# Gate splits on VectorE, down projections a step sooner, and next-layer inputs at the head of a step

## The chip, the cores and the metric

The kernel runs on one NeuronCore of a Trainium2 chip. The metric is the device time of one execution in microseconds. Three runs of the kernel before gave 650.26, 651.15 and 651.91 us, so the median is 651.15 us.

## What is computed

Local attention over blocks is followed by two feed-forward layers without a residual path. The first layer gates with a cosine, the second with Mish:

```python
def _moe_ref(x, w_in, w_out):          # layer 1 of the kernel's l = 0
    h = x @ w_in                        # 1536 x 512 @ 512 x 2048
    g = h * np.cos(h)
    return g @ w_out                    # 2048 x 512

def _moe2_ref(x, w_in, w_out):          # l = 1
    h = x @ w_in
    sp = np.where(h > 20.0, h, np.log1p(np.exp(np.minimum(h, 20.0))))
    return (h * np.tanh(sp)) @ w_out

x = attention(q, k, v)                  # 2 batches, 8 heads, 768 tokens, 64 wide
out = _moe2_ref(_moe_ref(x, ...), ...)
```

The attention part ends some 120 us after the start and is the same in both kernels.

## The kernel before

**Numbers in two halves.** TensorE multiplies in a rounded 32-bit format, so every operand is kept as a rounded upper half and a lower half, which is the value minus the upper half. Each product is made of three matmuls: upper by upper, lower by upper, upper by lower. The layer input X has the halves `xh` and `xl`, the weights `wih`, `wil`, `woh`, `wol`, and the gated activations `gh` and `gl`.

**Stages and steps.** A layer's 2048 hidden columns are cut into 4 groups `g` of 512, and the 1536 tokens into 3 blocks `j` of 512. A stage is one layer, group and block, so there are 24 stages: 0 to 11 for layer 0, 12 to 23 for layer 1. A stage has 4 tiles `f` of 128 hidden columns, so there are 96 tiles, and the loop over `k` in `layers()` makes one step per tile. In step k TensorE runs `up(k)`, 12 matmuls (L139) that make h of the tile in one of four banks, and then one `down(s, u)`, 12 matmuls (L555) that multiply the four gated tiles of a finished stage s with a quarter u of the output weights. A down needs all four `gh` and `gl` of its stage; the eleventh of its matmuls is the one that reads the last tile's `gl`.

**The gate of layer 0** spreads over two steps. In step k, `turns` makes n on ScalarE (L521) and r on VectorE in two instructions (L522, L523). In step k + 1, `cos_gate` takes the sine on ScalarE (L527) and multiplies on VectorE (`gg`, L529), and `split` makes `gh` on ScalarE (L514) and `gl` (L515). In layer 0 `gl` is made on GpSimd, in layer 1 on VectorE.

**Downs and what follows them.** When the last tile of a stage is split in step k, its four downs go into the list `downs` with a due step, k + 2 in layer 0 and k + 1 in layer 1 (`LAG`), and `do_down` takes one per step. In the step after a down, `do_after` adds its bank into `acc`, on ScalarE for g = 0 (L562) and on VectorE otherwise (L564). For the last group (g = 3), an `end` runs one step later still: in layer 0 it makes `xh` (L569, ScalarE) and `xl` (L570, GpSimd), which are the input of layer 1, and in layer 1 it stores the result.

**Weights for the next group** arrive meanwhile, eight chunks per group of 12 steps. The weights are 64-bit numbers, and each chunk is narrowed by one ScalarE instruction (L101) and three VectorE instructions (L105, L108, L111) in one step, and split in the next step by ScalarE (L121) and GpSimd (L122, `wil` or `wol`). Eight steps in twelve carry this load on VectorE; they are called heavy below, the others plain.

**The order** on each engine is the order of the program, written out by hand; nothing reorders it. One step issues on VectorE: `gg` of the tile before, the add, the two r of this tile, then the three narrowing instructions. Tile 43, for instance, is the last of stage 10; its `gg` is made in step 44 and written gg(43) below.

Of the kernel before, what the change touches and what calls it, by code (L numbers as in the profile page):

```python
# [9 lines left out]
F32 = mybir.dt.float32  # L10
# [4 lines left out]
ALU = mybir.AluOpType  # L15
# [5 lines left out]
def kernel(  # L21
# [11 lines left out]
    nc = tc.nc  # L33
# [8 lines left out]
    KD = DM // 128  # L42
# [5 lines left out]
    TPB = TB // 128  # L48
# [78 lines left out]
    stages = [(l, g, j) for l in range(2) for g in range(NG) for j in range(NBLK)]  # L127
    tiles = [(s, f) for s in range(len(stages)) for f in range(GF)]
    HP = {}

    def up(k, half=None):
        s, f = tiles[k]
        l, g, j = stages[s]
        w = W[l, g][0]
        ps = HP[k] = BANK[k % 4][:, 0:TB]
        n = 6 if half == 1 else 0
        for c in range(KD) if half is None else range(2 * half, 2 * half + 2):
            for a, e in PASS:
                nc.tensor.matmul(ps, lhsT=w[a][:, c, 128 * f:128 * f + 128],  # L139
                                 rhs=X[e][:, c, TB * j:TB * j + TB], start=(n == 0), stop=(n == 3 * KD - 1))  # L140
                n += 1
# [359 lines left out]
    def layers():  # L501
        with ExitStack() as es:
            gp = es.enter_context(tc.tile_pool(name="g", bufs=10))
            tp = es.enter_context(tc.tile_pool(name="tmp", bufs=3))
            ap = es.enter_context(tc.tile_pool(name="acc", bufs=NBLK))
            G, ACC = {}, {}

            def tmp(nm, bufs=3, dt=F32):
                return tp.tile([128, TB], dt, tag=nm, name=nm, bufs=bufs)

            def split(g, eng):

                hi, lo = [gp.tile([128, TB], F32R, tag="g" + a, name="g" + a) for a in "hl"]
                nc.scalar.copy(hi, g)  # L514
                eng.tensor_tensor(out=lo, in0=g, in1=hi.bitcast(F32), op=ALU.subtract)  # L515
                return hi, lo

            def turns(h):

                n, r = tmp("n", 2, I32), tmp("r")  # L520
                nc.scalar.activation(out=n, in_=h, func=AF.Identity, scale=1.0 / TWO_PI, bias=b_quarter)  # L521
                nc.vector.scalar_tensor_tensor(out=r, in0=n, scalar=-C1, in1=h, op0=ALU.mult, op1=ALU.add)  # L522
                nc.vector.scalar_tensor_tensor(out=r, in0=n, scalar=-C2, in1=r, op0=ALU.mult, op1=ALU.add)  # L523
                return h, r

            def cos_gate(h, r):
                nc.scalar.activation(out=r, in_=r, func=AF.Sin, bias=b_hpi)  # L527
                g = tmp("gg")
                nc.vector.tensor_tensor(out=g, in0=r, in1=h, op=ALU.mult)  # L529
                return g  # L530

            def mish(h):
                g = tmp("gg")
                nc.scalar.activation(out=g, in_=h, func=AF.Mish)  # L534
                return split(g, nc.vector)

            turn = [0]

            def dbank():
                turn[0] += 1  # L540
                return BANK[4 + turn[0] % 4]

            def down(s, u, d0=0, d1=DM):
                l, g, j = stages[s]
                w = W[l, g][1]
                if l == 0:
                    ps = dbank()[:, 0:TB]
                    mm = [(w[a][:, f, 128 * u:128 * u + 128], G[s, f][e]) for f in range(GF) for a, e in PASS]
                    col = slice(TB * u, TB * u + TB)
                else:  # L550
                    ps = dbank()[:, 0:d1 - d0]
                    mm = [(G[s, f][a][:, 128 * u:128 * u + 128], w[e][:, f, d0:d1]) for f in range(GF) for a, e in PASS]
                    col = slice(DM * u + d0, DM * u + d1)
                for n, (x, y) in enumerate(mm):
                    nc.tensor.matmul(ps, lhsT=x, rhs=y, start=(n == 0), stop=(n == len(mm) - 1))  # L555
                if u == 0 and g == 0:
                    ACC[l, j] = ap.tile([128, KD * TB], F32, tag="acc", name="acc")
                acc = ACC[l, j][:, col]

                def add():  # L560
                    if g == 0:
                        nc.scalar.copy(acc, ps)  # L562
                    else:
                        nc.vector.tensor_tensor(out=acc, in0=acc, in1=ps, op=ALU.add)  # L564

                def end():
                    if l == 0:
                        hi, lo = (y[:, u, TB * j:TB * j + TB] for y in X)
                        nc.scalar.copy(hi, acc)  # L569
                        nc.gpsimd.tensor_tensor(out=lo, in0=acc, in1=hi.bitcast(F32), op=ALU.subtract)  # L570
                    else:
                        r0 = TB * j + 128 * u
                        nc.sync.dma_start(out=out[r0:r0 + 128, d0:d1], in_=acc)

                return [add, end] if g == NG - 1 else [add]

            downs, after = [], [[], []]
            LAG = (2, 1)

            def do_after():  # L580
                now = after.pop(0)
                after.append([])
                for op in now:
                    op()

            def do_down(k):
                if downs and downs[0][0] <= k:
                    for x, op in zip(after, down(*downs.pop(0)[1:])):
                        x.append(op)

            def made(k, i, g):

                s, f = G_OF = tiles[i]
                G[G_OF] = g
                if f == GF - 1:
                    downs.extend((k + LAG[stages[s][0]], s, u) for u in range(KD if stages[s][0] == 0 else TPB))
                    if s == len(stages) - 1:
                        downs[-1:] = [(k, s, TPB - 1, 256 * h, 256 * h + 256) for h in range(2)]

            st = {}  # L600
            for k in range(len(tiles) + 12):
                if k < len(tiles):
                    if k not in HP:
                        up(k)
                    h = HP.pop(k)
                g = cos_gate(*st.pop(k - 1)) if k - 1 in st else None
                do_after()
                first = k < len(tiles) and stages[tiles[k][0]][0] == 0
                if first:
                    st[k] = turns(h)  # L610
                if g is not None:
                    made(k, k - 1, split(g, nc.gpsimd if first else nc.vector))
                if k < len(tiles) and not first:
                    made(k, k, mish(h))
                for op in WSEQ.get(tiles[k] if k < len(tiles) else None, ()):
                    op()
                do_down(k)
                if k >= len(tiles):
                    do_down(k + 99)
            do_after()  # L620
            do_after()

    groups = [(l, g) for l in range(2) for g in range(NG)]
    WSEQ = {}
# [26 lines left out]
    with tc.manual_schedule():  # L651
        def filler(i):
            for op in AT.get(i, ()):
                op()
            if NS <= i < NS + 6:
                up((i - NS) // 2, (i - NS) % 2)
        attention(filler)
        layers()
# [30 lines left out]
```

## Time and profile before

| | us |
|---|---|
| median of 3 runs | 651.15 |
| the profiled execution | 650.98 |
| its span, first to last instruction | 649.2 |
| outside the span | 1.8 |
| TensorE busy | 632.3 (97%) |
| VectorE busy | 440.9 (68%) |
| ScalarE busy | 320.2 (49%) |
| GpSimd busy | 236.8 (36%) |

The busy time of TensorE counts overlapping matmuls as they are pipelined, so 97% says only that there is nearly always a matmul in flight. What TensorE loses shows in two ways: as idle time ahead of a matmul, with the engine that ended it, and as fewer matmuls in a stretch of equal length. VectorE's 68% is a mean over layer 0, where it is busy nearly all the time, and layer 1, where it is not. Rows of the trace name an engine, a line of the kernel, the operation, what it writes and reads, and after a bracket how long the engine was idle and who ended that.

### The profile page before, as it was taken

The page shows a single profiled execution, that of the slowest core. Times are in us where ns is not written, and L with a number is a line of the kernel's source. Part 1 is how long each engine was busy: PE and PEld are TensorE (multiplying, and loading weights), DVE is VectorE, ACT ScalarE, POOL GpSimd, SP SyncE. Part 2 cuts the span into 40 slices and gives each one's busy share as a digit, 9 for nine tenths or more (in the row PEclk, how much of TensorE's full clock was granted, in tenths as well). Part 3 has the DMA queues.
Part 4 walks back from the last instruction along what each step waited for, and adds up shares of the span by engine and source line. Part 5 has one row for each costly group of instructions (what it writes and reads, how often), then busy time and mean ns, then how long its engine had stood idle before and what let it go on. Part 6 is the DMA issues. An engine that isn't in the chain of part 4 may idle for free.

```text
span 649.2 us, 8827 instructions
## 1 busy us (share of the span) xinstructions
PE 632.3 (97%) x3096; PEld 515.1 (79%) x3097; DVE 440.9 (68%) x813; ACT 320.2 (49%) x701; POOL 236.8 (36%) x279
## 2 busy tenths in 40 slices
PE   9998999999999999999999699999999999999998
PEld 4766778888878888888888588888888888888886
DVE  5698986488988989998999848622563366322222
ACT  5787897565565445544545545543543244322210
POOL 5466568255555443544355624310221022100000
PEclk9999999999999999999999799999999999999999
DMA  9969652022213211221122102311221122000112
GB/s 184 205 158 212 146 140 67 2 65 91 76 61 98 89 41 34 96 97 34 46 86 78 53 28 74 116 43 34 80 101 47 32 72 92 1 0 1 48 50 97
DMA packets 54410, 49.88 MB, mean 77 GB/s; under 512 B 44270, under 2 KB 44526, under 8 KB 54126
## 3 DMA queue, kind: packets, MB, share of 16 engines
q1 hardware_dynamic: 54366, 49.32, 27.2%
q8 instruction: 24, 0.39, 0.3%
q14 instruction: 20, 0.16, 0.1%
HBM read 45.57 MB, written 3.15 MB: 75 GB/s over the span
## 4 chain that ended last, share of the span: by engine, by line
PE 55%; DVE 32%; issue 6%; ACT 5%; POOL 1%; DMA 1%; DVEq 0%; ACTq 0%; POOLq 0%
PE bank L555 23%; PE bank L139 21%; PE bank L210 11%; DVE wx L105 6%; DVE wx L108 6%; DVE gg L529 4%; DVE r L523 4%; DVE r L522 3%; DVE acc L564 3%; DVE wx L111 2%; ACT r L527 1%; ACT wx L101 1%; DMA wst<-in_moe_w_in_dram 1%; ACT wih L121 1%; DVE vb L210 1%
## 5 line engine op out<-in xcount | busy, mean ns | idle before, releaser
L139 PE MATMUL bank<-xh,wih 128*128 128x512 f32 x384 | 150.6, 392 | 4.4 <-ACT xh L569 4.4
L139 PE MATMUL bank<-xl,wih 128*128 128x512 f32 x384 | 149.8, 390 | 0.6 <-POOL xl L570 0.6
L139 PE MATMUL bank<-xh,wil 128*128 128x512 f32 x384 | 149.7, 390 | 0.0
L515 POOL TENSOR_TENSOR gl<-gg,gh 128x512 fp32r<-128x512 f32 x47 | 67.8, 1442 | 132.6 <-ACT gh L514 106.6
L515 DVE TENSOR_TENSOR gl<-gg,gh 128x512 fp32r<-128x512 f32 x49 | 34.2, 697 | 115.2 <-ACT gh L514 115.1
L534 ACT ACTIVATE gg<-bank 128x512 f32<-128x512 f32 x48 | 28.7, 598 | 149.3 <-PE bank L139 147.9
L514 ACT CAST gh<-gg 128x512 fp32r<-128x512 f32 x96 | 59.6, 621 | 75.7 <-DVE gg L529 74.2
L139 PEld LDWEIGHTS bank<-xh,wih 128*128 128x128 f32 x384 | 72.2, 188 | 20.1 <-ACT xh L569 4.8
L139 PEld LDWEIGHTS bank<-xl,wih 128*128 128x128 f32 x384 | 72.2, 188 | 15.8 <-POOL xl L570 1.1
L139 PEld LDWEIGHTS bank<-xh,wil 128*128 128x128 f32 x384 | 72.2, 188 | 15.0
L122 POOL TENSOR_TENSOR wil<-wx,wih 128x512 fp32r<-128x512 f32 x32 | 46.4, 1450 | 88.8 <-ACT wih L121 84.6
L555 PE MATMUL bank<-gl,woh 128*128 128x512 f32 x192 | 75.7, 394 | 1.3 <-POOL gl L515 1.1
L105 DVE TENSOR_SCALAR wx<-wx 128x512 int32<-128x512 int32 x64 | 66.8, 1043 | 13.5 <-ACT wx L101 13.5
L555 PE MATMUL bank<-gh,woh 128*128 128x512 f32 x192 | 75.4, 393 | 0.0
L555 PE MATMUL bank<-wol,gh 128*128 128x512 f32 (+1 forms) x196 | 75.4, 385 | 0.0
L555 PE MATMUL bank<-woh,gl 128*128 128x512 f32 (+1 forms) x196 | 75.4, 385 | 0.0
L555 PE MATMUL bank<-woh,gh 128*128 128x512 f32 (+1 forms) x196 | 75.4, 385 | 0.0
L555 PE MATMUL bank<-gh,wol 128*128 128x512 f32 x192 | 75.3, 392 | 0.0
L210 POOL TENSOR_TENSOR pn<-pb,rs 128x256 f32<-128x256 f32 (+3 forms) x120 | 53.7, 472 | 38.2 <-PE bank L210 14.1
L564 DVE TENSOR_TENSOR acc<-acc,bank 128x512 f32<-128x512 f32 (+1 forms) x73 | 49.3, 675 | 26.0 <-PE bank L555 26.0
L122 POOL TENSOR_TENSOR wol<-wx,woh 128x512 fp32r<-128x512 f32 x32 | 47.3, 1477 | 49.4 <-ACT woh L121 40.8
L108 DVE SCALAR_TENSOR_TENSOR wx<-wst,wx 128x512 int32<-128x512 int32 x64 | 62.3, 973 | 1.9
(78 smaller groups left out, 1004.2 us busy)
## 6 DMA issues: line engine op xcount, KB each, us to landing
wst<-in_moe_w_in_dram SPq DMA_DIRECT2D x32, 512.0 KB, 3.5
wst<-in_moe_w_out_dram SPq DMA_DIRECT2D x32, 512.0 KB
kn<-in_k_dram SPq DMA_DIRECT2D x16, 192.0 KB, 4.0
qn<-in_q_dram SPq DMA_DIRECT2D x16, 192.0 KB, 3.8
vn<-in_v_dram SPq DMA_DIRECT2D x16, 192.0 KB, 3.1
out_dram<-acc SPq DMA_DIRECT2D x11, 256.0 KB, 2.0
vb<-in_v_dram SPq DMA_DIRECT2D x2, 960.0 KB, 7.4
vt<-in_v_dram SPq DMA_DIRECT2D x32, 18.8 KB, 3.0
```

What stands on the lines that cost most here:

```text
L105: nc.vector.tensor_scalar(out=xi, in0=xi, scalar1=3, scalar2=0x7FFFFFF8, op0=ALU.logical_shift_left, op1=ALU.bitwise_and)
L108: nc.vector.scalar_tensor_tensor(out=xi, in0=word[:, :, 0], scalar=29, in1=xi, op0=ALU.logical_shift_right, op1=ALU.bitwise_or)
L122: nc.gpsimd.tensor_tensor(out=lo, in0=x, in1=hi.bitcast(F32), op=ALU.subtract)
L139: nc.tensor.matmul(ps, lhsT=w[a][:, c, 128 * f:128 * f + 128], rhs=X[e][:, c, TB * j:TB * j + TB], start=(n == 0), stop=(n == 3 * KD - 1))
L210: todo[phase].append(lambda: fn(*a, **kw))
L514: nc.scalar.copy(hi, g)
L515: eng.tensor_tensor(out=lo, in0=g, in1=hi.bitcast(F32), op=ALU.subtract)
L523: nc.vector.scalar_tensor_tensor(out=r, in0=n, scalar=-C2, in1=r, op0=ALU.mult, op1=ALU.add)
L529: nc.vector.tensor_tensor(out=g, in0=r, in1=h, op=ALU.mult)
L534: nc.scalar.activation(out=g, in_=h, func=AF.Mish)
L555: nc.tensor.matmul(ps, lhsT=x, rhs=y, start=(n == 0), stop=(n == len(mm) - 1))
L564: nc.vector.tensor_tensor(out=acc, in0=acc, in1=ps, op=ALU.add)
```

## The change

Three things change in `layers()`.

- `split` makes `gl` on VectorE always, so in layer 0 it leaves GpSimd and stands on VectorE behind the two r of the step.
- The downs of stage 0 keep their two steps' distance; those of all other stages are due from one step behind the last split (`late`), each with its own due step, and up to two that are due run in a step. Stage 1 becomes due while the last down of stage 0 does, so step 9 has two downs, and from there on layer 0 is one down ahead of before. Step 52, at the border of the layers, has two as well, and layer 1 is then two downs ahead of before until its end.
- `do_after` is parted: the adds stay behind `gg`, and the ends go to the head of the step, ahead of the sine.

```diff
-            def split(g, eng):
+            def split(g):
                 hi, lo = [gp.tile([128, TB], F32R, tag="g" + a, name="g" + a) for a in "hl"]
                 nc.scalar.copy(hi, g)
-                eng.tensor_tensor(out=lo, in0=g, in1=hi.bitcast(F32), op=ALU.subtract)
+                nc.vector.tensor_tensor(out=lo, in0=g, in1=hi.bitcast(F32), op=ALU.subtract)
                 return hi, lo
...
-            downs, after = [], [[], []]
-            LAG = (2, 1)
-            def do_after():
-                now = after.pop(0)
-                after.append([])
-                for op in now:
+            downs, adds, ends = [], [], [[], []]
+            def do_adds():
+                while adds:
+                    adds.pop(0)()
+            def do_ends():
+                for op in ends.pop(0):
                     op()
-            def do_down(k):
-                if downs and downs[0][0] <= k:
-                    for x, op in zip(after, down(*downs.pop(0)[1:])):
-                        x.append(op)
+                ends.append([])
+            def do_downs(k):
+                for _ in range(2):
+                    if downs and downs[0][0] <= k:
+                        add, *end = down(*downs.pop(0)[1:])
+                        adds.append(add)
+                        ends[1].extend(end)
...
-                    downs.extend((k + LAG[stages[s][0]], s, u) for u in range(KD if stages[s][0] == 0 else TPB))
+                    late = 2 if s == 0 else 1
+                    downs.extend((k + late + u, s, u) for u in range(KD if stages[s][0] == 0 else TPB))
                     if s == len(stages) - 1:
-                        downs[-1:] = [(k, s, TPB - 1, 256 * h, 256 * h + 256) for h in range(2)]
+                        downs[-1:] = [(k + TPB, s, TPB - 1, 256 * h, 256 * h + 256) for h in range(2)]
...
                     h = HP.pop(k)
+                do_ends()
                 g = cos_gate(*st.pop(k - 1)) if k - 1 in st else None
-                do_after()
+                do_adds()
...
-                    made(k, k - 1, split(g, nc.gpsimd if first else nc.vector))
+                    made(k, k - 1, split(g))
...
-                do_down(k)
-                if k >= len(tiles):
-                    do_down(k + 99)
+                do_downs(k if k < len(tiles) else k + 99)
```

On VectorE, step 6, a heavy one of stage 1, before:

```order
L529 TENSOR_TENSOR gg<-r,bank_59 128x512
L522 SCALAR_TENSOR_TENSOR r<-n,bank_60 128x512
L523 SCALAR_TENSOR_TENSOR r<-n,r 128x512
L105 TENSOR_SCALAR wx<-wx 128x512
L108 SCALAR_TENSOR_TENSOR wx<-wst,wx 128x512
L111 SCALAR_TENSOR_TENSOR wx<-wst,wx 128x512
L529 TENSOR_TENSOR gg<-r,bank_60 128x512
```

and step 6 after the change:

```order
L529 TENSOR_TENSOR gg<-r,bank_59 128x512
L522 SCALAR_TENSOR_TENSOR r<-n,bank_60 128x512
L523 SCALAR_TENSOR_TENSOR r<-n,r 128x512
L515 TENSOR_TENSOR gl<-gg,gh 128x512
L105 TENSOR_SCALAR wx<-wx 128x512
L108 SCALAR_TENSOR_TENSOR wx<-wst,wx 128x512
L111 SCALAR_TENSOR_TENSOR wx<-wst,wx 128x512
L529 TENSOR_TENSOR gg<-r,bank_60 128x512
```

`gl` now stands between the second r and the narrowing, where VectorE had nothing of it before.

On TensorE at the end of step 9, where the last down of stage 0 (bank_62) ends, before:

```order
L555 MATMUL bank_62<-gh,woh 128x512
L555 MATMUL bank_62<-gl,woh 128x512
L555 MATMUL bank_62<-gh,wol 128x512
L139 MATMUL bank_60<-xh,wih 128x512
L139 MATMUL bank_60<-xl,wih 128x512
L139 MATMUL bank_60<-xh,wil 128x512
```

and after, where the first down of stage 1 (bank_63) follows at once and `up(10)` (bank_60) comes 12 matmuls later:

```order
L555 MATMUL bank_62<-gh,woh 128x512
L555 MATMUL bank_62<-gl,woh 128x512
L555 MATMUL bank_62<-gh,wol 128x512
L555 MATMUL bank_63<-gh,woh 128x512
L555 MATMUL bank_63<-gl,woh 128x512
L555 MATMUL bank_63<-gh,wol 128x512
```

From here on every down of layer 0 stands one place sooner among the ups than before.

On ScalarE, steps 46 and 47 before (n of step 46 reads bank_60, n of step 47 bank_61); the second `xh` is the last of token block 0 (stage 9, u = 3), which `up(48)`, the first of layer 1, reads:

```order
L101 ACTIVATE wx<-wst 128x512
L527 ACTIVATE r<-r,b_hpi 128x512
L569 CAST xh<-acc 128x512
L521 ACTIVATE n<-bank_60,b_quarter 128x512
L514 CAST gh<-gg 128x512
L121 CAST woh<-wx 128x512
L527 ACTIVATE r<-r,b_hpi 128x512
L569 CAST xh<-acc 128x512
L521 ACTIVATE n<-bank_61,b_quarter 128x512
```

and after, step 45 and the head of step 46, where the second `xh` is that same last one:

```order
L569 CAST xh<-acc 128x512
L527 ACTIVATE r<-r,b_hpi 128x512
L521 ACTIVATE n<-bank_59,b_quarter 128x512
L514 CAST gh<-gg 128x512
L121 CAST woh<-wx 128x512
L101 ACTIVATE wx<-wst 128x512
L569 CAST xh<-acc 128x512
L527 ACTIVATE r<-r,b_hpi 128x512
L521 ACTIVATE n<-bank_60,b_quarter 128x512
```

The last `xh` of the block moved from step 47, behind the sine, to step 46, ahead of it.

## Rows read from the trace of the kernel before

**Rows 1.** Groups by line: matmuls with xh and with gl; idle before, and releaser.

```profile
L139 PE MATMUL bank<-xh,wih 128*128 128x512 f32 x384 | 150.6, 392 | 4.4 <-ACT xh L569 4.4
...
L555 PE MATMUL bank<-gl,woh 128*128 128x512 f32 x192 | 75.7, 394 | 1.3 <-POOL gl L515 1.1
```

**Rows 2.** Busy time by stretch (PE, PEld, DVE, ACT, POOL), PEclk, DMA: attention, layers' border.

```profile
60.00:80.00 20.00, 17.11 (x124) 13.54 (x120) 17.49 (x69) 16.71 (x59) 10.38 (x21) 0.91 0.62 141
...
360.00:380.00 20.00, 15.07 (x55) 11.58 (x54) 13.85 (x18) 10.51 (x17) 10.54 (x8) 0.83 0.09 26
380.00:400.00 20.00, 20.00 (x90) 16.57 (x89) 13.60 (x17) 9.42 (x17) 7.22 (x5) 1.00 0.19 55
...
366.10:373.00 6.90, 5.42 (x12) 3.94 (x13) 5.46 (x7) 4.48 (x8) 4.52 (x4) 0.51 0.00 0
```

**Rows 3.** Timeline at the border: start, length, engine, line, out<-in, idle before.

```profile
363.01 0.68 DVE L564 TENSOR_TENSOR acc<-acc,bank 128x512 f32<-128x512 f32 x1
...
366.36 0.60 ACT L569 CAST xh<-acc 128x512 fp32r<-128x512 f32 x1
...
367.02 0.79 PE L139 MATMUL bank<-xh,wih 128*128 128x512 f32 x1 [4.36 <-ACT xh L569]
...
368.38 0.79 PE L139 MATMUL bank<-xl,wih 128*128 128x512 f32 x1 [0.57 <-POOL xl L570]
```

**Rows 4.** Timeline, VectorE in a plain step of layer 0.

```profile
239.20 0.69 DVE L529 TENSOR_TENSOR gg<-r,bank 128x512 f32<-128x512 f32 x1 [0.86 <-ACT r L527]
...
241.12 1.34 DVE L523 SCALAR_TENSOR_TENSOR r<-n,r 128x512 f32<-128x512 int32 x1
...
243.32 0.69 DVE L529 TENSOR_TENSOR gg<-r,bank 128x512 f32<-128x512 f32 x1 [0.86 <-ACT r L527]
```

**Rows 5.** Timeline, VectorE and GpSimd in a heavy step of layer 0.

```profile
270.62 0.68 DVE L529 TENSOR_TENSOR gg<-r,bank 128x512 f32<-128x512 f32 x1
...
272.53 1.40 DVE L523 SCALAR_TENSOR_TENSOR r<-n,r 128x512 f32<-128x512 int32 x1
273.86 1.52 DVE L105 TENSOR_SCALAR wx<-wx 128x512 int32<-128x512 int32 x1
...
276.75 0.68 DVE L529 TENSOR_TENSOR gg<-r,bank 128x512 f32<-128x512 f32 x1
...
272.09 1.30 POOL L515 TENSOR_TENSOR gl<-gg,gh 128x512 fp32r<-128x512 f32 x1 [3.12 <-issue]
273.35 1.74 POOL L122 TENSOR_TENSOR wil<-wx,wih 128x512 fp32r<-128x512 f32 x1
```

**Rows 6.** Timeline, the same VectorE operations where no GpSimd operation was running ahead.

```profile
178.48 0.69 DVE L523 SCALAR_TENSOR_TENSOR r<-n,r 128x512 f32<-128x512 int32 x1
...
250.62 0.41 DVE L105 TENSOR_SCALAR wx<-wx 128x512 int32<-128x512 int32 x1
...
378.08 0.69 DVE L515 TENSOR_TENSOR gl<-gg,gh 128x512 fp32r<-128x512 f32 x1 [1.90 <-ACT gh L514]
```

**Rows 7.** Timeline, gg of tile 7 and the first matmul of down(1, 0).

```profile
154.01 0.68 DVE L529 TENSOR_TENSOR gg<-r,bank 128x512 f32<-128x512 f32 x1
...
154.68 0.39 PE L555 MATMUL bank<-gh,woh 128*128 128x512 f32 x1
```

**Rows 8.** Timeline, steps 44 to 46: matmuls behind up(44) and up(46), VectorE before gg(43).

```profile
341.41 0.39 PE L555 MATMUL bank<-gh,woh 128*128 128x512 f32 x1
...
345.75 1.72 DVE L108 SCALAR_TENSOR_TENSOR wx<-wst,wx 128x512 int32<-128x512 int32 x1
...
348.11 0.68 DVE L529 TENSOR_TENSOR gg<-r,bank 128x512 f32<-128x512 f32 x1
...
352.29 0.39 PE L555 MATMUL bank<-gh,woh 128*128 128x512 f32 x1
```

**Rows 9.** Timeline, TensorE behind two other idle times.

```profile
62.31 0.85 PE L210 MATMUL bank<-ident,pn 128*128 128x128 f32 x3 [2.06 <-ACT pt L210]
...
180.35 0.50 PE L555 MATMUL bank<-gl,woh 128*128 128x512 f32 x1 [1.07 <-POOL gl L515]
```

More of the change, by code (lines that the diff above doesn't have):

```diff
@@ L534, in mish @@
                 nc.scalar.activation(out=g, in_=h, func=AF.Mish)
-                return split(g, nc.vector)
+                return split(g)
             turn = [0]
@@ L616, in layers @@
                     op()
-                do_down(k)
-                if k >= len(tiles):
-                    do_down(k + 99)
-            do_after()
-            do_after()
+                do_downs(k if k < len(tiles) else k + 99)
+            do_adds()
+            do_ends()
+            do_ends()
     groups = [(l, g) for l in range(2) for g in range(NG)]
```

## Prediction

> **What bounds the kernel now.** I read the groups by line first, for TensorE's idle time in the layers and who ends it. There are only two places [rows 1]: 4.4 us ahead of a matmul with xh, and 1.3 us in all ahead of matmuls with gl. Then the busy time by stretch, for what the first place costs: from 360 to 380 us TensorE ran 55 matmuls, from 380 to 400 us 90 [rows 2]. The 35 missing ones, at 20 / 90 = 0.222 us, are 7.8 us. That is more than the idle time, because from 366.1 to 373 us the granted clock is 0.51, the level of 1.2 GHz, after it had been at 2.4 GHz until TensorE stood idle [rows 2]. Everywhere else in the layers TensorE runs at its pace: a step is 24 matmuls, and (352.29 - 341.41) / 2 = 5.44 us [rows 8], so half a step, an up or a down, is 2.72 us.
>
> The timeline then shows why TensorE stood idle [rows 3]. up(48) needs the last xh and xl of token block 0. VectorE's add of that part is at 363.01, the end with xh on ScalarE at 366.36, one step later and behind a sine, and TensorE goes on at 367.02 and, with xl, at 368.38. So VectorE is late, not TensorE. Its own pace shows in two kinds of step. From gg to gg a heavy step takes 276.75 - 270.62 = 6.13 us [rows 5], over TensorE's 5.44; a plain one takes 243.32 - 239.20 = 4.12 us, 0.86 of it waiting for the sine [rows 4]. Eight heavy and four plain steps are 65.5 us against 12 x 5.44 = 65.3 us. VectorE is level with TensorE over a group and runs behind it by a few us, until the extra GpSimd work of the ends makes heavy steps longer and the border comes.
>
> **What gl on VectorE costs.** It adds 0.69 us to each of 47 steps [rows 6]. What it takes away is in the lengths of other VectorE instructions. The second r takes 0.69 us alone [rows 6], but 1.34 to 1.40 where GpSimd's gl started just before it [rows 4, 5]; L105 takes 0.41 alone [rows 6] and 1.52 under GpSimd's wil [rows 5]. In both cases the VectorE instruction ends some 0.3 to 0.55 us behind GpSimd's: it waits until GpSimd is done. So two GpSimd operations in a heavy step hold VectorE up by 0.71 + 1.11 = 1.8 us. With gl gone from GpSimd one operation of about 1.3 us is left to hold up one VectorE instruction, about 1.1 us, and gl adds 0.7: 1.8 us again. A heavy step stays near 6.1 us. In a plain step no GpSimd operation is left, so the second r is 0.65 us shorter, and gl fits into the 0.86 us in which VectorE waits for the sine. That makes 4.12 - 0.65 = 3.45 us. Four plain steps win 2.6 us per group, so VectorE catches up with TensorE in each group and starts the heavy steps without delay.
>
> The Trainium skill (GPSIMD Engine Reference, section 1) says that GpSimd shares its memory interfaces with VectorE and contends with VectorE instructions that have two inputs in SBUF. The new gl is such an instruction. By that rule it can itself be held up by the weights' split; the trace agrees as far as the second r goes.
>
> **The downs a step sooner.** The count of matmuls is the same, so this costs only where a down now comes before its gl. The eleventh matmul of a down reads the last gl, 2.27 us after the first.
>
> Stage 1: down(1, 0) began at 154.68 [rows 7]; now up(10) is behind it, so it begins at 151.96 and wants gl at 154.2. gg(7) was at 154.01 [rows 7]. Steps 4 to 7 each save up to about 0.4 us (L105 1.1 shorter, gl 0.7 longer), so gg(7) lies between 152.4 and 154.0. gl follows behind two r: gg, r, r and gl without hindrance end 2.6 us after gg begins, and 3.7 us after if wil comes first. gl is then ready between 155.0 and 157.7, and TensorE waits 0.8 to 3.5 us; I take 1.8, nearer the low end because L105's saving is measured. Once TensorE is that much later, stage 2 fits almost: 0.1.
>
> Stages 3 to 9: VectorE starts each group level. Stage 7 is the tightest. From step 27, where VectorE is level, five heavy steps are 5.8 + 4 x 6.1 = 30.2 us against 5 x 5.44 = 27.2, so gg(31) begins 3.0 us behind the end of up(32). gl comes 4.4 us later (one add more than above, wil first), at 7.4; down(7, 0) follows up(33), so it is wanted at 5.44 + 2.27 = 7.7. That is about even; I take 0.1, bounds 0 and 0.5.
>
> Stage 10: the ends of stage 9 add xl to GpSimd, and L108 is 1.72 us there [rows 8], about 1.1 more per step. Before, gg(43) began 348.11 - 341.41 = 6.7 us behind up(44). Now, level at step 39, five heavy steps, two of them longer, are 3 x 6.0 + 2 x 7.2 = 32.4 us against 27.2, so gg(43) begins 5.2 us behind up(44), and gl is there 3.3 to 4.4 us later, at 8.5 to 9.6. down(10, 0) follows up(45), so its gl is wanted at 5.44 + 2.27 = 7.7. TensorE waits 0.8 to 1.9 us; if VectorE is not level at step 39, up to 3; I take 1.4. Behind that stall stage 11 has its gl in time.
>
> **The border of the layers.** The last down of stage 9 is in step 44, its add in step 45, its end at the head of step 46. With gg(44) 7.2 us behind gg(43), the end's xh is made some 2.4 us after gg(44), ahead of the sine, and xl behind one wol, about 5.7 us after gg(44): 5.2 + 7.2 + 5.7 = 18.1 us behind up(44). up(48) wants it at 3 x 5.44 + 2.72 + 2.27 + 1.4 = 22.7. A margin of over 4 us: the wait goes, and with it the slow clock behind it. What is late next is gl for the downs, as above. In layer 1 a down comes two places sooner. There gh and gl follow the up within three instructions, and the down has another half step and an up before it; no cost. GpSimd's 47 operations of gl were beside other work but for the holding up already counted. The last matmuls and stores keep their order.
>
> **Sum.** Gone: 7.8 + 1.3 = 9.1 us. New: 1.8 + 0.1 + 0.1 + 1.4 = 3.4 us. 650.98 - 9.1 + 3.4 = 645.3 for the profiled execution, which holds the 649.2 us span and 1.8 us around it, neither of them touched outside the layers; it lies 0.17 under the median of 651.15, so 645.5 us.
>
> **Rivals.** (1) The clock falls in the new waits. Behind 4.36 us idle it was at 1.2 GHz for 6.9 us [rows 2, 3]. Behind 1.07 us the next matmul took 0.50 us against 0.79 at the border, so it held; behind 2.06 us in the attention [rows 9] it fell, since that stretch has 0.91 [rows 2]. Mine are 1.8 and 1.4. A fall like the border's costs 6.9 us x (1 - 0.51) = 3.3 us: 648.8 for one, 652 for two. The Trainium skill (TensorE: Matmul & The Clock Gate, What's actually happening) says that the slow clock is the default and that activity lifts it; the border's rows agree, and by that rule alone any new wait is suspect.
> (2) Slower: the second r and gl are both held up, or wil falls between them, so that gl costs its 0.7 us in heavy steps and nothing comes back. A heavy step is then 6.8 us, a group 8 x 6.8 + 4 x 3.45 = 68.2 us against 65.3, and VectorE sets layer 0: 4 x 2.9 = 11.6 us, with 1.8 at stage 1, less the 9.1: about 655.5. It decides from a heavy step of some 6.7 us. For it speaks that gl on VectorE never ran beside a weights' split in the trace; against it that two hold-ups become one.
> (3) No wait to speak of is left, gl coming first every time: 642 to 643.
> (4) The border's wait stays in part, because block 0's xl still queues on GpSimd behind the splits, or the edits cancel: about 650. The order speaks against it, since xh stands a whole step sooner.
>
> **How the numbers follow.** A measurement can tell about 0.3%, 2 us, from no change: faster is below 649.2, slower above 653.1. The forecast, 643.3 to 647.8, has 0.58; rival 3 0.10; rival 1 0.17, of which 0.12 below 649.2; rival 4 0.07; rival 2 0.08. So faster is 0.80, same 0.12, slower 0.08. The range runs from 642.3, into rival 3, to 649.5, over most of rival 1.
>
> **What would show it.** After: no idle ahead of matmuls with xh, 90 matmuls in each 20 us across the border, PEclk 1.00 there. TensorE's idle time ahead of matmuls with gl grows from 1.3 to about 3.4 us, now released by VectorE, at stages 1 and 10. Second r in plain steps 0.69 us, plain steps 3.5 us, heavy ones 6.1. I am wrong if heavy steps exceed 6.5 us, or if PEclk is under 1 near stages 1 or 10.

## The result and the profile after

The changed kernel takes 644.47 us (median of 4 runs, 644.08 to 645.08) against 651.53 us for the kernel before (4 runs, 650.26 to 652.07). The ratio is 0.9895, with a 95% interval of 0.9878 to 0.9912: 1.05% faster, about 7 us. The profiled execution took 644.43 us, with a span of 642.7 us. The 651.15 us given for the kernel before is the median of three of its four runs.

TensorE's groups by line in the changed kernel (busy, mean ns, then the idle time before them and who ended it), against [rows 1]:

```profile
L139 PE MATMUL bank<-xh,wih 128*128 128x512 f32 x384 | 150.2, 391 | 0.0
...
L555 PE MATMUL bank<-gl,woh 128*128 128x512 f32 x192 | 74.9, 390 | 2.1 <-DVE gl L515 2.1
```

The 4.4 us ahead of a matmul with xh are gone. The idle time ahead of matmuls with gl grew from 1.3 to 2.1 us and is now ended by VectorE. Busy time by stretch of the changed kernel (PE, PEld, DVE, ACT, POOL, PEclk, DMA), against [rows 2]:

```profile
140.00:160.00 20.00, 19.22 (x84) 15.45 (x83) 19.59 (x27) 11.41 (x21) 5.94 (x4) 1.00 0.28 87
...
340.00:360.00 20.00, 18.67 (x82) 15.14 (x82) 19.69 (x24) 10.26 (x18) 9.19 (x6) 1.00 0.24 80
360.00:380.00 20.00, 20.00 (x90) 16.54 (x89) 16.21 (x22) 11.80 (x19) 9.20 (x6) 1.00 0.08 26
```

Across the border, from 360 to 380 us, TensorE runs 90 matmuls instead of 55, at a granted clock of 1.00 instead of 0.83. What is left lies in the two other stretches. The timeline of TensorE in the changed kernel shows both places, with the first matmul of the waiting down and the first of the up that follows it, for the second place:

```profile
155.62 0.50 PE L555 MATMUL bank<-gl,woh 128*128 128x512 f32 x1 [0.78 <-DVE gl L515]
...
349.34 0.39 PE L555 MATMUL bank<-gh,woh 128*128 128x512 f32 x1
...
353.09 0.50 PE L555 MATMUL bank<-gl,woh 128*128 128x512 f32 x1 [1.33 <-DVE gl L515]
...
353.67 0.39 PE L139 MATMUL bank<-xh,wih 128*128 128x512 f32 x1
```

These are down(1, 0) and down(10, 0), the two that the prediction named. The second takes 353.67 - 349.34 = 4.33 us instead of 2.72, so an idle time of 1.33 us loses 1.6.

VectorE in a plain step of the changed kernel, against [rows 4], and in step 44 with the GpSimd work beside it, against [rows 5, 8]:

```profile
231.10 0.68 DVE L529 TENSOR_TENSOR gg<-r,bank 128x512 f32<-128x512 f32 x1
231.69 0.68 DVE L564 TENSOR_TENSOR acc<-acc,bank 128x512 f32<-128x512 f32 x1
232.29 0.68 DVE L522 SCALAR_TENSOR_TENSOR r<-n,bank 128x512 f32<-128x512 int32 x1
233.00 0.69 DVE L523 SCALAR_TENSOR_TENSOR r<-n,r 128x512 f32<-128x512 int32 x1
233.61 0.69 DVE L515 TENSOR_TENSOR gl<-gg,gh 128x512 fp32r<-128x512 f32 x1
234.49 0.69 DVE L529 TENSOR_TENSOR gg<-r,bank 128x512 f32<-128x512 f32 x1 [0.19 <-ACT r L527]
...
348.75 0.68 DVE L529 TENSOR_TENSOR gg<-r,bank 128x512 f32<-128x512 f32 x1
...
350.67 0.69 DVE L523 SCALAR_TENSOR_TENSOR r<-n,r 128x512 f32<-128x512 int32 x1
351.27 1.77 DVE L515 TENSOR_TENSOR gl<-gg,gh 128x512 fp32r<-128x512 f32 x1
352.96 1.51 DVE L105 TENSOR_SCALAR wx<-wx 128x512 int32<-128x512 int32 x1
...
350.69 1.81 POOL L122 TENSOR_TENSOR wol<-wx,woh 128x512 fp32r<-128x512 f32 x1 [3.59 <-DVE r L522]
352.46 1.73 POOL L570 TENSOR_TENSOR xl<-acc,xh 128x512 fp32r<-128x512 f32 x1
```

The plain step takes 3.39 us instead of 4.12: the second r is 0.69 us instead of 1.34, and gl fills most of the wait for the sine. In step 44 the split of weights begins 0.02 us behind the second r and comes ahead of gl, which takes 1.77 us instead of 0.69.

### The profile page after: what moved, and what is told of

Same layout as the page of the kernel before. It is cut to its first block, busy times and chain, and to the rows that moved or that the text cites. A ratio compares the mean times of both kernels' runs of the same rounds, so it can differ in the third digit from the quotient of the medians.

```text
span 642.7 us, 8804 instructions
## 1 busy us (share of the span) xinstructions
PE 629.9 (98%) x3096; PEld 514.2 (80%) x3097; DVE 443.4 (69%) x860; ACT 321.4 (50%) x701; POOL 177.5 (28%) x232
## 4 chain that ended last, share of the span: by engine, by line
PE 82%; DVE 12%; ACT 2%; DMA 1%; issue 1%; POOL 1%; ACTq 0%; DVEq 0%; POOLq 0%
PE bank L555 36%; PE bank L139 35%; PE bank L210 11%; DVE gl L515 2%; DVE r L523 2%; DVE wx L105 1%; DVE r L522 1%; DVE gg L529 1%; DVE wx L111 1%; DVE wx L108 1%; DMA wst<-in_moe_w_in_dram 1%; DVE vb L210 1%; DVE acc L564 1%; DVE pb L210 1%; DMA wst<-in_moe_w_out_dram 1%
## 5 line engine op out<-in xcount | busy, mean ns | idle before, releaser
L515 DVE TENSOR_TENSOR gl<-gg,gh 128x512 fp32r<-128x512 f32 x96 | 91.4, 952 | 114.9 <-ACT gh L514 114.9
L122 POOL TENSOR_TENSOR wil<-wx,wih 128x512 fp32r<-128x512 f32 x32 | 48.7, 1523 | 219.4 <-ACT wih L121 187.5
L122 POOL TENSOR_TENSOR wol<-wx,woh 128x512 fp32r<-128x512 f32 x32 | 49.7, 1552 | 113.1 <-ACT woh L121 52.3
L105 DVE TENSOR_SCALAR wx<-wx 128x512 int32<-128x512 int32 x64 | 55.1, 860 | 8.3 <-ACT wx L101 8.3
L521 ACT ACTIVATE n<-bank,b_quarter 128x512 int32<-128x512 f32 x48 | 32.8, 683 | 41.6 <-PE bank L139 41.6
L108 DVE SCALAR_TENSOR_TENSOR wx<-wst,wx 128x512 int32<-128x512 int32 x64 | 47.8, 747 | 1.9
```

The source lines that it names most:

```text
L105: nc.vector.tensor_scalar(out=xi, in0=xi, scalar1=3, scalar2=0x7FFFFFF8, op0=ALU.logical_shift_left, op1=ALU.bitwise_and)
L108: nc.vector.scalar_tensor_tensor(out=xi, in0=word[:, :, 0], scalar=29, in1=xi, op0=ALU.logical_shift_right, op1=ALU.bitwise_or)
L122: nc.gpsimd.tensor_tensor(out=lo, in0=x, in1=hi.bitcast(F32), op=ALU.subtract)
L515: nc.vector.tensor_tensor(out=lo, in0=g, in1=hi.bitcast(F32), op=ALU.subtract)
```

## Experiments

All times are medians; "waits" are TensorE's idle times inside the layers, from the profile. The experiments were run in three sets, each with runs of the kernel before beside it, and the ratios are taken within a set. The kernel before had medians of 651.26 us (first set, `e1` to `e4`), 651.48 (`e6`, `e8`, `e10`, `e11`) and 650.6 (`e5`, `e12`).

### Each edit alone

**gl on VectorE alone** (`e1_gl_only`), in the kernel before:

```diff
-                    made(k, k - 1, split(g, nc.gpsimd if first else nc.vector))
+                    made(k, k - 1, split(g, nc.vector))
```

> The kernel before with one edit: gl of layer 0 on VectorE. Downs and ends stay where they were. Theory (VectorE is what layer 0 was late on, and gl on VectorE takes more off it than it adds): plain steps 3.4 us, heavy ones 6.0, no wait for gl in layer 0, and at the border of the layers a wait of 1 to 2.5 us with the clock held at 1.00, so 642.5 to 645.5 us, most of the whole gain from this edit alone. Rival (the downs a step sooner make the gain, gl on VectorE costs 0.7 us a step and is paid by them): 650 us or more, the border's wait longer than 4.4 us.

Measured: 643.96 us, ratio 0.9897 (0.9877 to 0.9916). There is no wait for gl, and these two at the border (TensorE, timeline), in a stretch from 360 to 380 us with the clock at 1.00:

```profile
361.92 0.50 PE L139 MATMUL bank<-xh,wih 128*128 128x512 f32 x1 [0.64 <-ACT xh L569]
363.48 0.50 PE L139 MATMUL bank<-xl,wih 128*128 128x512 f32 x1 [1.06 <-POOL xl L570]
...
360.00:380.00 20.00, 18.31 (x80) 14.60 (x79) 13.89 (x19) 11.26 (x18) 8.92 (x6) 1.00 0.03 13
```

This one edit gives as much as all three together. The rival, that gl on VectorE is a cost paid by the downs, falls. The border waits less because VectorE comes sooner, and not because GpSimd has a shorter queue: in the kernel before TensorE waited mostly for xh [rows 3], which GpSimd does not make.

**The downs alone** (`e2_downs_only`): the change's `late` and `do_downs` in the kernel before, with

```diff
-                do_ends()
                 g = cos_gate(*st.pop(k - 1)) if k - 1 in st else None
                 do_adds()
+                do_ends()
...
-                    made(k, k - 1, split(g))
+                    made(k, k - 1, split(g, nc.gpsimd if first else nc.vector))
```

against the changed kernel.

> The kernel before with the downs of the change alone (stage 0 two steps off, the others one, two in step 9); gl of layer 0 on GpSimd, ends behind the adds as before. Theory: the border's wait is gone (block 0's last xl is ready some 4 us ahead of its matmul), but VectorE runs behind as before and GpSimd's gl comes later than VectorE's, so down(1, 0) waits about 3 us and down(2, 0) about 1: 645 to 647 us, up to 649 if the clock falls in the 3 us. Rival (this edit alone makes the gain): at most 644.5 us.

Measured: 647.74 us, ratio 0.9951 (0.9936 to 0.9967). No wait for xh or xl; TensorE waits instead for the gates, first in down(1, 0) and then in down(2, 0):

```profile
156.32 0.50 PE L555 MATMUL bank<-gh,woh 128*128 128x512 f32 x1 [1.23 <-ACT gh L514]
158.13 0.50 PE L555 MATMUL bank<-gl,woh 128*128 128x512 f32 x1 [1.31 <-POOL gl L515]
...
181.26 0.50 PE L555 MATMUL bank<-gl,woh 128*128 128x512 f32 x1 [1.05 <-POOL gl L515]
```

The waits are near those expected: 2.5 us, for about 3, and 1.05, for about 1. Two more, of 0.34 and 0.43 us, come at stages 10 and 11, and the time is 0.7 us above the upper end given for it without a fall of the clock. The clock stayed at 1.00 in these stretches.

**The ends alone** (`e3_ends_only`): the change's split lists with gl on GpSimd and

```diff
-                    late = 2 if s == 0 else 1
+                    late = 2 if stages[s][0] == 0 else 1
```

> The kernel before with the ends alone moved to the head of the step, ahead of the sine; gl of layer 0 on GpSimd, layer 0's downs two steps off (layer 1's take their distance of one step from step 53 on). Theory: xh is made 2 us sooner at the border, but xl is then behind a weights' split on GpSimd and hardly sooner, so TensorE waits first 2 and then 3 us: 648.5 to 651 us. Rival (the sine ahead of xh was what the border waited for): under 647 us, border wait under 2.5 us.

Measured: 650.24 us, ratio 0.9992 (0.9982 to 1.0003), no difference that can be measured. At the border xh is sooner and xl hardly is:

```profile
365.47 0.50 PE L139 MATMUL bank<-xh,wih 128*128 128x512 f32 x1 [1.96 <-ACT xh L569]
368.75 0.80 PE L139 MATMUL bank<-xl,wih 128*128 128x512 f32 x1 [2.77 <-POOL xl L570]
```

The two waits are 4.7 us together, against 4.9 in [rows 3]. The rival, that the border waited for the sine ahead of xh, falls.

### Each edit taken out of the change

**Without gl on VectorE** (`e4_after_gl_on_gpsimd`): the changed kernel with `split(g, nc.gpsimd if first else nc.vector)` for the cosine gate.

> The changed kernel with gl of layer 0 back on GpSimd. Theory: as with the downs alone, 645 to 647 us, because the ends' place does not matter once the downs are a step sooner. Rival (gl on VectorE is paid by the other edits): at most 644.0 us, below the changed kernel.

Measured: 646.5 us, ratio 0.9932 (0.9914 to 0.995): the waits of the downs alone again, 1.25 and 1.30 in down(1, 0), 1.06 in down(2, 0); the wait at stage 10 is 0.26 us and there is none at stage 11. The rival falls: gl's place is worth 2 us inside the change. This kernel differs from `e2_downs_only` only in the ends' place and is 1.2 us faster (646.06 to 646.83 against 647.5 to 648.02). In the two profiled executions 0.7 us of the difference lies in the layers, where the waits at stages 10 and 11 are the shorter ones, and 1.1 us lies ahead of the first down, which no edit touches. So with gl on GpSimd and the downs sooner the ends' place is worth up to some 0.7 us.

**Without the downs sooner** (`e5_no_downs_sooner`): `late = 2 if stages[s][0] == 0 else 1`, the rest as in the change.

> The changed kernel with all of layer 0's downs two steps off (gl on VectorE and the ends at the head kept; layer 1's downs one off from step 53 on). Theory: no wait for gl at stages 1 and 10; at the border xh is in time and xl, behind the split of weights on GpSimd, leaves a wait of 0 to 1.2 us: 641.8 to 643.8 us, below the changed kernel. Rival (the downs' earlier place is needed for the border even with gl on VectorE): a border wait of 1.7 us or more in all, 644 us or more.

Measured: 645.14 us (643.25 to 645.76), ratio 0.9906 (0.9883 to 0.9928). Here I was wrong, and the rival's numbers came: the border's wait is one of 1.97 us for xl, not 0 to 1.2, and the clock fell behind it (the matmul takes 0.64 us instead of 0.50, and the stretch has 0.91 instead of 1.00):

```profile
362.93 0.64 PE L139 MATMUL bank<-xl,wih 128*128 128x512 f32 x1 [1.97 <-POOL xl L570]
...
360.00:380.00 20.00, 18.03 (x73) 14.43 (x72) 12.93 (x18) 10.93 (x17) 8.59 (x6) 0.91 0.02 9
```

GpSimd's rows in that kernel show where xl's time goes; the second two are the same place in `e1_gl_only`, where everything is 0.54 us later from the attention on:

```profile
359.39 1.81 POOL L122 TENSOR_TENSOR wol<-wx,woh 128x512 fp32r<-128x512 f32 x1 [3.59 <-DVE r L522]
361.16 1.72 POOL L570 TENSOR_TENSOR xl<-acc,xh 128x512 fp32r<-128x512 f32 x1
```

```profile
359.93 1.81 POOL L122 TENSOR_TENSOR wol<-wx,woh 128x512 fp32r<-128x512 f32 x1 [3.59 <-DVE r L522]
361.94 1.48 POOL L570 TENSOR_TENSOR xl<-acc,xh 128x512 fp32r<-128x512 f32 x1 [0.20 <-ACT xh L569]
```

With the end at the head, xl stands directly behind wol, beside a gl on VectorE that is running until 361.76, and takes 1.72 us; with the end behind the sine it begins 0.24 us later, against the offset, and takes 1.48. It ends at 362.88 in the one and at 363.42 in the other, which less the offset of 0.54 is 362.88 again. The ends' place moves xh alone. It turns the two waits of `e1_gl_only`, 0.64 and 1.06 us, into one of 1.97, behind which the clock fell: from the first down to the last matmul the layers take 507.4 us here and 505.8 there. So gl on VectorE shortens the wait at the border but does not end it; the downs' earlier place ends it, and also makes two new waits.

**Without the ends at the head** (`e6_ends_behind_gg`):

```diff
-                do_ends()
                 g = cos_gate(*st.pop(k - 1)) if k - 1 in st else None
                 do_adds()
+                do_ends()
```

> The changed kernel with the ends back behind gg and the adds. Theory (the ends' place is not what freed the border; it only decides when xl hinders VectorE): no wait for xh or xl at the border, since the last xl is still some 6 us ahead of its matmul; the steps made longer by xl begin one step later, so the wait for gl at stage 10 falls from 1.33 us to 0.6 or less: 643.2 to 644.5 us. Rival (the place at the head freed the border): an idle time ahead of xh or xl of 2 us or more, 646 us or more.

Measured: 644.21 us, ratio 0.9893 (0.9878 to 0.9908), 0.3 us from the changed kernel, which is within the runs' spread. The border is free, as expected, and the rival falls. But the wait at down(10, 0) is 1.30 us, not 0.6: xl runs in the same steps of VectorE whether its end stands ahead of the sine or behind it, since wol is ahead of it in both. That part of my expectation was wrong.

### Which steps of gl count

**Plain steps only** (`e11_gl_in_plain_steps`) and **heavy steps only** (`e12_gl_in_heavy_steps`), both in the kernel before:

```diff
+            def heavy(k):
+                return 4 <= k <= 11 or (k >= 12 and 2 <= k % 12 <= 9)
...
-                    made(k, k - 1, split(g, nc.gpsimd if first else nc.vector))
+                    made(k, k - 1, split(g, nc.gpsimd if first and heavy(k) else nc.vector))
```

with `not heavy(k)` in the second.

> The kernel before with gl of layer 0 on VectorE only in the plain steps (no narrowing of weights); in the heavy steps on GpSimd; downs and ends as before. Theory (the gain of gl on VectorE is made in the plain steps, where GpSimd no longer holds VectorE up; in heavy ones it is nearly even): plain steps 3.4 us, heavy ones 6.1, a border wait of 2 to 3.5 us, waits for gl at stages 1 and 2 as before: 644.5 to 647 us. Rival (the heavy steps make it): 648.5 us or more, border wait over 4 us.

> The kernel before with gl of layer 0 on VectorE only in the heavy steps (those that narrow weights); in the plain steps on GpSimd; downs and ends as before. Theory (it is the plain steps that let VectorE catch up): plain steps 4.1 us, heavy ones 6.0 us or, in the first group, 5.4; the waits for gl at stages 1 and 2 are gone, but at the border a wait for xh of 3 us or more stays with the clock at half: 647.5 to 649.5 us. Rival (the heavy steps alone suffice, 0.1 us less in each being what counts): border wait under 2 us, under 646 us.

Measured: 646.53 us, ratio 0.9929 (0.9914 to 0.9943), for plain steps; 645.93 us, ratio 0.9921 (0.9901 to 0.994), for heavy ones. The border in the first, then in the second:

```profile
363.36 0.49 PE L139 MATMUL bank<-xh,wih 128*128 128x512 f32 x1 [1.35 <-ACT xh L569]
364.90 0.79 PE L139 MATMUL bank<-xl,wih 128*128 128x512 f32 x1 [1.05 <-POOL xl L570]
```

```profile
363.64 0.49 PE L139 MATMUL bank<-xh,wih 128*128 128x512 f32 x1 [1.35 <-ACT xh L569]
365.00 0.50 PE L139 MATMUL bank<-xl,wih 128*128 128x512 f32 x1 [0.86 <-POOL xl L570]
```

The plain steps did what was expected, but for the wait at stage 2, 0.55 us instead of the 1.07 of before. The heavy steps did more: I expected a wait for xh of 3 us or more and at least 647.5 us; the waits are 1.35 and 0.86. The rival's time came, under 646 us by a hair, but not its wait of under 2. The lengths of the steps were the expected ones: in groups 1 to 3 a heavy step went from 6.07 to 6.13 us down to 6.01, and as long as the adds are those of the first group, on ScalarE, it went from 5.79 to 5.41. What was wrong is what they add up to. These are VectorE and GpSimd in a step of the first group of the changed kernel:

```profile
147.54 0.68 DVE L529 TENSOR_TENSOR gg<-r,bank 128x512 f32<-128x512 f32 x1
...
149.46 0.68 DVE L515 TENSOR_TENSOR gl<-gg,gh 128x512 fp32r<-128x512 f32 x1
150.06 1.52 DVE L105 TENSOR_SCALAR wx<-wx 128x512 int32<-128x512 int32 x1
151.62 0.69 DVE L108 SCALAR_TENSOR_TENSOR wx<-wst,wx 128x512 int32<-128x512 int32 x1
...
152.96 0.68 DVE L529 TENSOR_TENSOR gg<-r,bank 128x512 f32<-128x512 f32 x1
...
149.47 1.83 POOL L122 TENSOR_TENSOR wil<-wx,wih 128x512 fp32r<-128x512 f32 x1 [3.59 <-ACT wih L121]
```

gl begins 0.01 us ahead of wil here, so it is not held up, and L105 alone waits for GpSimd. In `e12_gl_in_heavy_steps` eleven such steps (5 to 11 and 15 to 18) save 0.37 us each, some 4 us in all. Whether VectorE has caught up shows on ScalarE, ahead of n, the first operation of a gate: n then waits for TensorE. In the kernel before it doesn't do so once between 130 us and the border. It does with the plain steps alone, and with the heavy ones alone:

```profile
308.39 0.69 ACT L521 ACTIVATE n<-bank,b_quarter 128x512 int32<-128x512 f32 x1 [1.95 <-PE bank L139]
```

```profile
308.67 0.69 ACT L521 ACTIVATE n<-bank,b_quarter 128x512 int32<-128x512 f32 x1 [1.46 <-PE bank L139]
```

So either kind of step is enough for VectorE to be level some 55 us ahead of the border, and what is left of the border's wait, 2.2 to 2.4 us, arises behind that point. Both kernels still have the slow clock behind it: the stretch from 360 to 380 us has 0.91. How much of the first group's 4 us counts at the border was not tried by itself.

### What the earlier downs are needed for

**Stages 0 to 2 two steps off** (`e8_three_stages_two_off`):

```diff
-                    late = 2 if s == 0 else 1
+                    late = 2 if s <= 2 else 1
```

> The changed kernel with stages 0, 1 and 2 two steps off instead of stage 0 alone, caught up at stage 3. Theory (stage 1 waits because VectorE has had no chance to catch up by then): no wait ahead of step 40, since VectorE is level at steps 14 to 17; the wait of 1.33 us at stage 10 stays: 642.8 to 643.8 us. Rival (the first stage that is one step off waits, whichever it is): a wait of 0.7 us or more at down(3, 0), 644.3 us or more.

Measured: 642.89 us, ratio 0.9873 (0.9856 to 0.9891). The wait at down(1, 0) is gone and none came at stage 3; down(10, 0) waits 1.30 us. The rival falls: stage 1 waited because VectorE had not caught up by then.

**Stage 9 alone a step sooner** (`e10_stage9_alone_sooner`):

```diff
-                    late = 2 if s == 0 else 1
+                    late = 1 if s == 9 or stages[s][0] == 1 else 2
```

> The changed kernel with only stage 9's downs one step off in layer 0 (two downs in step 41, none in step 45); all other stages of layer 0 two steps off as before, layer 1's one off from step 53 on. Theory (all that the downs' earlier place was needed for is block 0's last xh and xl; everywhere else it only brings gl nearer to its use): no idle time ahead of any matmul of the layers, 641.0 to 642.5 us, below the changed kernel. Rival (the earlier place also keeps VectorE's adds and the border's other blocks in time): a wait at the border or at stage 10 stays, 643.5 us or more.

Measured: 641.19 us (641.05 to 641.28), ratio 0.9849 (0.9834 to 0.9863). Groups by line and the stretches of that kernel:

```profile
L139 PE MATMUL bank<-xh,wih 128*128 128x512 f32 x384 | 150.2, 391 | 0.0
...
L555 PE MATMUL bank<-gl,woh 128*128 128x512 f32 x192 | 74.7, 389 | 0.0
...
340.00:360.00 20.00, 20.00 (x90) 16.57 (x89) 19.69 (x23) 9.52 (x17) 10.54 (x6) 1.00 0.22 73
360.00:380.00 20.00, 20.00 (x90) 16.56 (x89) 16.05 (x22) 13.89 (x23) 7.63 (x6) 1.00 0.14 43
```

TensorE has no idle time left in the layers, and the rival falls. It beats the changed kernel by 3.3 us with a change of one line: the earlier place was needed for block 0's last xh and xl, and everywhere else it only brought a down nearer to its gl.

## Why the prediction was right, point by point

**The sum** came out at 645.5 us and the kernel at 644.47. The profiled executions differ by 650.98 - 644.43 = 6.55 us where 5.7 were forecast. `e10_stage9_alone_sooner`, which waits nowhere in the layers, allows each side of the sum to be measured. From the first down to the last matmul the layers take 513.6 us before, 506.4 after and 503.5 there. So the kernel before loses 10.1 us to waits and the slow clock, where the sum has 9.1, and the changed kernel 2.9, where it has 3.4. Both errors make the gain too small, by 1.5 us together; the attention part (below) hides 0.6 of that. That the time came within 1 us is in part luck; the terms themselves are right in kind and size.

**The border** went as worked out, 7.8 us and the slow clock with it. In the changed kernel the last xh is made from 358.18, and xl at 359.55 takes 1.74 us; its matmul is at 366.83, a margin of 5.5 us, where over 4 were forecast. But the step that put this down to the earlier downs, with gl on VectorE only making VectorE level, told half of it. `e1_gl_only` has a border wait of 1.7 us instead of 4.9 with the downs untouched, and `e2_downs_only` has none with gl untouched: either removes most of it, and so their gains don't add. The third edit does nothing measurable alone (`e3_ends_only`) or inside the change (`e6_ends_behind_gg`); in the two settings between, it gained up to 0.7 us in one (`e4_after_gl_on_gpsimd` against `e2_downs_only`) and cost 1.6 in the layers in the other, by way of the clock (`e5_no_downs_sooner` against `e1_gl_only`, one profiled execution each, and their times overlap).

**What gl costs on VectorE.** The plain step was forecast at 3.45 us and took 3.39; the heavy step at 6.1 and took 6.01. That one hold-up of VectorE would take the place of two is in the rows of such a step of the changed kernel, with VectorE's add in it:

```profile
217.37 1.78 DVE L515 TENSOR_TENSOR gl<-gg,gh 128x512 fp32r<-128x512 f32 x1
219.08 0.42 DVE L105 TENSOR_SCALAR wx<-wx 128x512 int32<-128x512 int32 x1
...
216.79 1.82 POOL L122 TENSOR_TENSOR wol<-wx,woh 128x512 fp32r<-128x512 f32 x1 [4.19 <-DVE r L522]
```

gl is held up here by 1.1 us, and L105 no more, as the sum had it; GpSimd's operation, taken at about 1.3 us, lasts 1.8. The heavy steps with the first group's adds, 0.37 us shorter each, went only into stage 1 (up to 0.4 us each, rightly).

**The new waits** were forecast at 1.8 us at down(1, 0), 1.4 at down(10, 0), and 0.1 at two others; they were 0.78, 1.33 and none. At stage 10 the case with wol ahead of gl came true, and at stage 1 the case without: gg(7) at 152.96, which is 152.3 without the 0.6 us that this execution's attention part took longer, came at the lower of the bounds of 152.4 and 154.0, and gl was ready 2.6 us later. I had taken a value between the two cases for the one place and for the other; at down(1, 0) that made the forecast 1.0 us of idle time too long.

**Waits lose more than their idle time.** Taking the waits for gl at their idle time was a little low, for the old and the new alike: down(10, 0) loses 1.6 us to 1.33 of idle time, and the layers of `e8_three_stages_two_off`, with that wait alone, take 1.6 us longer than those of `e10_stage9_alone_sooner`.

**Rivals.** The clock did not fall behind waits of 0.78 and 1.33 us, so the first rival didn't come; in `e5_no_downs_sooner` it did behind 1.97. The second, VectorE slowing layer 0, would have needed heavy steps of 6.7 us. The third, no wait to speak of, did not come in the change, but `e10_stage9_alone_sooner` shows that it was to be had, at 641.19 us. The fourth, a wait left at the border, did not come either. The Trainium skill's rule (GPSIMD Engine Reference, section 1) that VectorE instructions with two inputs in SBUF contend with GpSimd holds for gl too: it takes 0.69 us alone and 1.77 behind wol. L105 has one input and is held up as well, 0.41 us against 1.52, which the rule as the prediction gives it does not cover.

**The attention part**, the same in both, differed between these two executions: the first down of layer 0 began at 132.55 us before and at 133.19 after. So 0.6 us of the layers' gain doesn't show in the difference of the two times.

## What to carry to other kernels

Where an engine is late and the one that waits is not, first ask what holds the late engine up: here a helper's instruction on GpSimd cost VectorE about as much as doing that work itself, so taking it over was nearly free in the steps that were full and a gain in the others. Work that is moved forward in the order to meet one deadline should move only where that deadline is; everywhere else it shortens somebody's slack. Edits that remove the same wait don't add up, and only a run of each alone shows which one did it.

## What the runs showed of the hardware that was not expected

- When VectorE's and GpSimd's operations collide, it matters who is under way. gl that began within 0.02 us of wil, ahead of it or behind it, took 0.68 to 0.69 us, and wil 1.8 (changed kernel, wil at 149.47, 193.88 and 199.32 us); gl that began 0.6 us behind wol took 1.77. Once set, the order stayed step after step. GpSimd's subtraction took 1.3 us when a VectorE instruction of two inputs had 0.1 us left to run at its start, 1.74 when it had 0.6 left and 1.8 when the two began together.
- Idle times of one size differ in what the clock does after them. It stayed at 2.4 GHz behind 1.23 and 1.31 us with one matmul between (`e2_downs_only`), and behind 0.64 and 1.06 (`e1_gl_only`); it fell to 1.2 GHz behind 1.35 and 1.05 (`e11_gl_in_plain_steps`, the matmul of 0.79 us), behind 1.35 and 0.86 (`e12_gl_in_heavy_steps`, from 365.8 us) and behind 1.97 alone (`e5_no_downs_sooner`). What decides between 2.5 us that held and 2.0 to 2.4 us that fell stays open here. Each fall lasted about 3.5 us, and 6.9 in the kernel before.
